# Keys of the first four groups loaded as whole rows, and scores issued one group ahead

## The chip, the cores and the metric

The kernel runs on one core of a Trainium2 chip. The metric is device time in microseconds (us), 1071.01 us before the change: the median of 3 runs.

## The reference, cut to what matters

Chunked attention with 8 memory keys feeds two MLPs, all in float32:

```python
for c in range(24):                                  # chunks of 32 queries, 4 batches, 8 heads
    q_c = q[:, :, 32*c : 32*c + 32]
    k_ctx = k[:, :, max(0, 32*c - 16) : min(768, 32*c + 40)]
    v_ctx = v[:, :, max(0, 32*c - 16) : min(768, 32*c + 40)]
    s = concat([mem_k, k_ctx]) @ q_c / 8             # 8 memory keys, then up to 56 of the context
    a = exp(s - max(s)); a = a / (sum(a) + 1e-9)
    out[:, :, 32*c : 32*c + 32] = a @ concat([mem_v, v_ctx])
x = out as (3072, 512)
h = x @ w_in;   x = (h - tanh(h)) @ w_out            # 512 -> 2048 -> 512
h = x @ w_in2;  g = h if h >= 1, 0 if h <= -1, else (h + 1)**2 / 4;  out = g @ w_out2
```

## The kernel before, in words

**Attention.** The 96 chunks are worked in 24 groups of 4, so a group has 128 queries. For one group, *scores* (`att_scores`, L393) are 64 small matmuls on PE, from queries (128x4x128) and 4 sets of 64 keys. *max* (L411 to L418, DVE) subtracts each row's maximum, *exp* (L428, ACT) follows, *sum* (L445 to L447, DVE) adds up and inverts. *transposes* (L453, PE) and *at* (L458, ACT) turn the probabilities over, *values* (L467, PE) multiplies by V, *norm* (L477, DVE) scales, and *x* (L487, PE) turns the result over into a PSUM tile `start_tx`. From there *xh* (L493, ACT) takes the fp32r high part and *xl* (L498, DVE) the remainder. Scores and values of a group share a PSUM tile `start_a`; transposes and x share `start_tx`.

**Keys.** A chunk's row in DRAM (`qkv_t`) has, for 128 partitions and 4 pairs of heads, 128 keys: 8 memory keys and 120 of the context, of which its own window is the first 64 (8 + 16 + 32 + 8). The rows were laid out with 72 keys to the right, so that a row also holds the windows of the next two chunks, 32 and 64 keys further on. Before, only the first 64 are loaded: one load a chunk, 128 KB, four pieces of 256 bytes a partition (L364).

**The MLPs.** Each matrix product is made of three fp32r products (high times high, high times low, low times high). *hidden* (L563) of one step is 12 matmuls, 4 for each product; *gate* is L576 (ACT) and L577 (DVE); *output* is L601. The weights arrive as float64, a tile of 128x512 pairs of integers (512 KB) in one of four buffers `stage_0` to `stage_3`, and are turned to float32 on the way: *act* (ACT, L138 makes `raw`, L141 shifts the low word), *mag* (DVE, L147 and L148), *sign* (DVE, L156, and the add of POOL, L161), then *whi* (ACT, L173) and *wlo* (DVE, L180). Weight tile 4 goes where tile 0 was, so its load waits for POOL's add of weight 0; tile 5 waits for that of weight 1, and so on.

**The order around the change.** The engines run what they are given in the written order. The *start section* comes first: 11 fills (`warm(WARM, fill)`, L1040: 128x512 bf16 matmuls on zeros into an unused tile), then four groups, one after the other (`for j in range(PER)`, PER = 4), and between their stages the rounding of weights 0 to 3 and more fills (`KEEP`: 6 behind the scores, 2 behind the transposes, 2 behind the values of groups 0 to 2, and the scores of a next group behind its values). In group 3 the first hidden product starts on the 384 columns of groups 0 to 2 (`EARLY_N`), in three parts between the stages of group 3. Behind the start section the main loop takes one hidden step after the other, and group 4 (`att_load`, scores, exp and so on) lies beside its first steps. SP issues all loads in written order: queries and keys of a group, a weight tile, the values, and so on. Each load takes one of 8 semaphores in turn.

## Time and profile before

| what | value |
|---|---|
| runs | 1071.01, 1071.11, 1069.24 us; median 1071.01 |
| span of the profiled execution | 1070.1 us (the page has no time of it beside the span) |
| instructions | 21112 |
| busy | PE 98%, PEld 80%, DVE 80%, ACT 61%, POOL 4% |
| chain that ended last | PE 93%, DMA 2%, SP's queue 2%, ACT 1%, DVE 1% |

The busy share says which engine has no room over the whole span. The chain goes back from the last instruction, at each step to what released it: where it names an engine, that engine's time is in the total; where it names a transfer or a queue, work stood still for it.

### The profile page before, as it was taken

What the parts mean: (1) busy time and instruction counts of PE and PEld (TensorE: products, weight loads), DVE (VectorE), ACT (ScalarE), POOL (GpSimd) and SP (SyncE); (2) the same over time, 40 slices, a digit from 0 to 9 for tenths busy, and PEclk for the clock granted to TensorE, in tenths of its full rate; (3) what the DMA queues carried; (4) which work ended last, traced back from release to release, by engine and by line L of the source; (5) the groups of instructions that cost most, each with busy time, mean ns of one, the idle gap of its engine ahead of it and who ended that gap; (6) DMA issues with size and microseconds to landing.
All of it is one profiled execution on the core that took longest, in us unless ns stands there. A gap on an engine that the chain in (4) does not pass through costs nothing.

```text
span 1070.1 us, 21112 instructions
## 1 busy us (share of the span) xinstructions
PE 1052.4 (98%) x7589; PEld 859.7 (80%) x7589; DVE 855.7 (80%) x1511; ACT 650.0 (61%) x1203; POOL 42.7 (4%) x38
## 2 busy tenths in 40 slices
PE   7799999999999999999999999999999999999998
PEld 3577888888888888888888888888888888888887
DVE  4898987877799999999999778698477787476854
ACT  2687756555455565565566677757477666577553
POOL 0232212000000000000000000000000000000000
PEclk9999999999999999999999999999999999999999
DMA  8999887898889999876487978787766877766774
GB/s 207 245 258 247 260 240 207 258 292 272 266 269 315 325 302 292 292 261 205 154 278 263 313 221 259 210 277 214 232 194 195 261 224 232 214 194 195 203 203 146
DMA packets 212088, 259.37 MB, mean 242 GB/s; under 512 B 65424, under 2 KB 129168, under 8 KB 211984
## 3 DMA queue, kind: packets, MB, share of 16 engines
q1 hardware_dynamic: 211840, 257.88, 80.2%
q8 instruction: 61, 1.00, 0.4%
q14 instruction: 43, 0.35, 0.1%
q10 hardware_dynamic: 144, 0.13, 0.0%
HBM read 199.23 MB, written 58.72 MB: 241 GB/s over the span
## 4 chain that ended last, share of the span: by engine, by line
PE 93%; DMA 2%; SPq 2%; ACT 1%; DVE 1%; issue 0%; ACTq 0%
PE h L563 23%; PE acc L893 21%; PE acc L601 17%; PE qa L805 12%; PE qc L805 6%; PE qb L805 3%; PE acc_-1_1_7132 L893 2%; PE acc_-1_0_7131 L893 2%; DMA stage<-w_in 2%; PE a L467 1%; SPq L364 1%; PE a L393 1%; PE acc_-1_1_7508 L893 1%; PE acc_-1_0_7507 L893 1%; PE b L487 1%; PE b L453 1%
## 5 line engine op out<-in xcount | busy, mean ns | idle before, releaser
L893 PE MATMUL acc<-ghi,inG 128*128 128x512 f32 x672 | 183.0, 389 | 0.0
L576 ACT ACTIVATE g<-h 128x512 f32<-128x512 f32 x96 | 57.7, 601 | 176.7 <-PE h L563 154.9
L893 PEld LDWEIGHTS acc<-ghi,inG 128*128 128x128 f32 x672 | 126.2, 188 | 26.1
L227 DVE TENSOR_TENSOR glo<-g,ghi 128x512 fp32r<-128x512 f32 x174 | 117.8, 688 | 27.4 <-ACT ghi L226 26.3
L805 PE MATMUL qa<-xc,inP 128*128 128x512 f32 x576 | 139.3, 389 | 0.0
L226 ACT ACTIVATE ghi<-g 128x512 fp32r<-128x512 f32 x174 | 107.3, 627 | 43.6 <-DVE glo L227 21.1
L805 PEld LDWEIGHTS qa<-xc,inP 128*128 128x128 f32 x576 | 108.1, 188 | 22.4
L563 PE MATMUL h<-xh,whi 128*128 128x512 f32 (+2 forms) x388 | 105.6, 394 | 3.9 <-DVE g L577 1.9
L893 PE MATMUL acc<-glo,inG 128*128 128x512 f32 x336 | 107.0, 389 | 0.1
L563 PE MATMUL h<-xl,whi 128*128 128x512 f32 (+2 forms) x388 | 104.0, 390 | 0.1
L563 PE MATMUL h<-xh,wlo 128*128 128x512 f32 (+2 forms) x388 | 103.8, 389 | 0.0
L577 DVE TENSOR_TENSOR g<-h,g 128x512 f32<-128x512 f32 x96 | 66.0, 688 | 38.7 <-ACT g L576 38.1
L563 PEld LDWEIGHTS h<-xh,whi 128*128 128x128 f32 x388 | 71.5, 188 | 21.2 <-issue 4.1
L743 ACT ACTIVATE t<-g,half 128x512 f32<-128x512 f32 x72 | 52.2, 725 | 59.1 <-DVE g L739 59.1
L563 PEld LDWEIGHTS h<-xl,whi 128*128 128x128 f32 x388 | 73.0, 189 | 15.2 <-DVE xl L498 0.2
L563 PEld LDWEIGHTS h<-xh,wlo 128*128 128x128 f32 x388 | 72.1, 188 | 14.7
L180 DVE TENSOR_TENSOR wlo<-raw,whi 128x512 fp32r<-128x512 f32 x112 | 80.7, 720 | 0.0
L173 ACT ACTIVATE whi<-raw 128x512 fp32r<-128x512 f32 x112 | 70.5, 630 | 6.5 <-POOL raw L161 6.5
L601 PE MATMUL acc<-ghi,whi 128*128 128x512 f32 x256 | 74.0, 403 | 0.0
L893 PEld LDWEIGHTS acc<-glo,inG 128*128 128x128 f32 x336 | 63.0, 188 | 13.5 <-DVE glo L227 0.5
L805 PE MATMUL qc<-xc,inP 128*128 128x512 f32 x288 | 73.1, 389 | 0.0
L601 PE MATMUL acc<-ghi,wlo 128*128 128x512 f32 x256 | 70.7, 390 | 0.0
(717 smaller groups left out, 1811.3 us busy)
## 6 DMA issues: line engine op xcount, KB each, us to landing
inP<-part SPq DMA_DIRECT2D x168, 256.0 KB, 3.0
inG<-part SPq DMA_DIRECT2D x168, 256.0 KB, 3.0
stage<-w_in SPq DMA_DIRECT2D x32, 512.0 KB, 6.0
stage<-w_out SPq DMA_DIRECT2D x32, 512.0 KB, 5.5
part<-preph SPq DMA_DIRECT2D x64, 256.0 KB, 4.6
whi<-w1o SPq DMA_DIRECT2D x48, 256.0 KB, 4.9
wlo<-w1o SPq DMA_DIRECT2D x48, 256.0 KB, 5.1
part<-prepl SPq DMA_DIRECT2D x48, 256.0 KB, 4.7
```

The costliest lines, as they stand in the source:

```text
L173: nc.scalar.activation(out=hi, in_=r, func=AF.Copy)
L180: nc.vector.tensor_tensor(out=lo, in0=r, in1=hi.bitcast(F32), op=ALU.subtract)
L226: nc.scalar.activation(out=hi, in_=src, func=AF.Copy)
L227: nc.vector.tensor_tensor(out=lo, in0=src, in1=hi.bitcast(F32), op=ALU.subtract)
L364: nc.sync.dma_start(out=k[j // 2][:, j % 2], in_=ks[j, :, :, :WIN])
L563: nc.tensor.matmul(hp, w[:, kc * 128:(kc + 1) * 128], x[:, kc, n0:n1], start=j == 0 and kc == 0, stop=j == 2 and kc == KC - 1,)
L576: nc.scalar.activation(out=g, in_=hp, func=AF.Tanh)
L577: nc.vector.tensor_tensor(out=g, in0=hp, in1=g, op=ALU.subtract)
L601: nc.tensor.matmul(acc_t[dm], w[:, dm * 128:(dm + 1) * 128], g, start=first and j == 0, stop=last and j == 2,)
L743: nc.scalar.activation(out=t, in_=h, func=AF.Relu, scale=0.5, bias=half)
L805: nc.tensor.matmul(o, w[:, k * 128:(k + 1) * 128], z[k], start=i in (1, 2, 5) and j == 0 and k == 0, stop=j == 2 and k == 1, skip_group_ch ...
L893: nc.tensor.matmul(bank[a][c], w[:, c * 128:(c + 1) * 128], g, start=first and j == 0, stop=last and j == 2, skip_group_check=True,)
```

## The change

The loads of keys of groups 0 to 3 are replaced by 6 loads of whole rows (chunks 0, 3, 6, 9, 12 and 15; 256 KB each, 2 KB a partition in one piece). The chunk of a row reads its window in place. For the other ten chunks GpSimd (POOL) copies the 8 memory keys and the 56 context keys out of a row into a set of 64 (`att_windows`, two copies a chunk, 128x4x8 and 128x4x56; sets in `prep0` to `prep4`).

The loop over the four groups is written anew: scores of group j + 1 stand right behind the transposes of group j, its max before the values of j, its exp behind them. There is one tile `start_tx` for all groups instead of one a group, and two `start_a`. Four fills stand behind the values of groups 0 to 2 in the place of ten. Weight 0 is rounded on DVE behind the norm and the xl of group 2, and its whi is made in group 3.

```diff
-KEEP = {"s": 6, "t": 2, "v": 2}
+REACH = (KEYS - WIN) // CHUNK + 1
+KEEP = 4
...
+            att_v(t, (free.pop(0), free.pop(0)))
+            return
+        q = free.pop(0).rearrange("p (j a c) -> p j a c", j=GC, a=NPAIR)
+        nc.sync.dma_start(out=..., in_=qkv[t * GC:(t + 1) * GC, :, :NPAIR * TQ]...)
+        for c in range(t * GC, (t + 1) * GC):
+            if c % REACH == 0:
+                k = free.pop(0)
+                nc.sync.dma_start(out=k, in_=qkv[c, :, NPAIR * TQ:QK])
+                k_rows.append(k.rearrange("p (a c) -> p a c", a=NPAIR))
...
+    def att_windows(t):
+        keys = []
+        for c in range(t * GC, (t + 1) * GC):
+            m, u = divmod(c, REACH)
+            if len(k_win) <= m:
+                k_win.append(slot(f"prep{m}", f"startk{m}").rearrange("p (u a c) -> p u a c", u=2, a=NPAIR))
+            if u:
+                w = k_win[m][:, u - 1]
+                nc.gpsimd.tensor_copy(out=w[:, :, :NMEM], in_=k_rows[m][:, :, :NMEM])
+                nc.gpsimd.tensor_copy(
+                    out=w[:, :, NMEM:], in_=k_rows[m][:, :, NMEM + u * CHUNK:NMEM + u * CHUNK + WIN - NMEM]
+                )
+                keys.append(w)
+            else:
+                keys.append(k_rows[m][:, :, :WIN])
+        st[t]["k"] = keys
...
-    start_scores(0)
+    start_a = [pool.tile([128, 2, 512], F32, tag=tag, name=f"start_a{i}") for i, (pool, tag) in ...]
+    start_tx = ps_acc.tile([128, 2, 512], F32, tag="acc1", name="start_tx")
+    att_windows(0)
+    att_scores(0, start_a[0])
+    att_max(0)
+    att_exp(0)
     for j in range(PER):
         last = j == PER - 1
+        att_transpose(j, start_tx[:, 0, :])
         if not last:
-            warm(KEEP["s"], fill)
-        att_max(j)
-        if j:
-            att_xl(j - 1)
+            att_windows(j + 1)
+            att_scores(j + 1, start_a[(j + 1) % 2])
+        att_at(j)
+        att_sum(j)
         if last:
+            split_weights_hi(0, 0)
+            round_mag(0, 0, 1)
             split_weights_lo(0, 0)
-            hidden(0, 0, EARLY_N, (0,))
-        if 1 < j:
-            round_sign(0, 0, j - 2)
-        att_exp(j)
-        att_sum(j)
-        tx = ps_acc.tile([128, 2, 512], F32, tag="acc1", name=f"start_tx{j}")
-        att_transpose(j, tx[:, 0, :])
-        att_at(j)
-        if j == 2:
-            split_weights_hi(0, 0)
-        if j:
-            round_act(0, 0, j - 1)
-        if last:
-            split_weights_hi(1, 0)
-            hidden(0, 0, EARLY_N, (1,))
+            hidden(0, 0, EARLY_N, (0, 1))
+            round_sign(0, 0, 1)
         else:
-            warm(KEEP["t"], fill)
-        att_values(j, st_pair.pop(j))
+            att_max(j + 1)
+        att_values(j, start_a[j % 2])
         if last:
             hidden(0, 0, EARLY_N, (2,))
         else:
-            warm(KEEP["v"], fill)
-            start_scores(j + 1)
+            att_exp(j + 1)
+            warm(KEEP, fill)
         att_norm(j)
-        if last:
-            split_weights_lo(1, 0)
-        if j:
-            round_mag(0, 0, j - 1)
-        att_x(j, tx[:, 1, :])
+        if j == 2:
+            round_mag(0, 0, 0)
+        att_x(j, start_tx[:, 1, :])
         att_xh(j)
-    att_xl(PER - 1)
-    round_sign(0, 0, 2)
+        if 0 < j:
+            round_act(0, 0, j - 1)
+        att_xl(j)
+        if j == 2:
+            round_sign(0, 0, 0)
+    split_weights_hi(1, 0)
+    split_weights_lo(1, 0)
+    round_rest(0, 0, 2)
     round_act(0, 0, 3)
     round_rest(0, 0, 3)
```

In the rows of order that follow, each instruction stands as line, operation, tile written, tiles read, shape and count; a number in a tile's name is a running number.

SP's queue before, the loads of groups 1 and 2 with their weight tiles (start_151 and start_156 are the queries, the 128x4x64 rows the keys, the 64x2x256 rows the values):

```order
L358 DMA start_151<-qkv_t 128x4x128
L364 DMA start_152<-qkv_t 128x4x64 x2
L364 DMA start_153<-qkv_t 128x4x64 x2
L126 DMA stage_0_180<-w_in 128x1024
L377 DMA start_154<-qkv_t 64x2x256 x2
L377 DMA start_155<-qkv_t 64x2x256 x2
L358 DMA start_156<-qkv_t 128x4x128
L364 DMA start_157<-qkv_t 128x4x64 x2
L364 DMA start_158<-qkv_t 128x4x64 x2
L126 DMA stage_1_191<-w_in 128x1024
L377 DMA start_159<-qkv_t 64x2x256 x2
```
and now (start_152 and start_156 are the rows of keys):

```order
L354 DMA start_151<-qkv_t 128x4x128
L361 DMA start_152<-qkv_t 128x512
L128 DMA stage_0_175<-w_in 128x1024
L407 DMA start_153<-qkv_t 64x2x256 x2
L407 DMA start_154<-qkv_t 64x2x256 x2
L354 DMA start_155<-qkv_t 128x4x128
L361 DMA start_156<-qkv_t 128x512
L128 DMA stage_1_183<-w_in 128x1024
L407 DMA start_157<-qkv_t 64x2x256 x2
L407 DMA start_158<-qkv_t 64x2x256 x2
```
Four loads of keys a group became one (two in groups 0 and 3); everything behind them is nearer to the front by as many places.

DVE before, from xl of group 2 to xl of group 3 (L498; r_587 is the sum, xn_643 the norm of group 3; raw_0 to raw_2 are weights 0 to 2):

```order
L498 TENSOR_TENSOR xl_355<-start_tx_481,xh_354 128x4x128
L180 TENSOR_TENSOR wlo_0_577<-raw_0_381,whi_0_488 128x512
L156 SCALAR_TENSOR_TENSOR raw_1_490<-stage_1_191,raw_1_490 128x512
L445 TENSOR_REDUCE r_587<-e_571 128x8
L446 TENSOR_SCALAR r_587<-r_587 128x8
L447 RECIPROCAL r_587<-r_587 128x8
L477 TENSOR_TENSOR xn_643<-start_a_529,r_587 128x512
L180 TENSOR_TENSOR wlo_1_645<-raw_1_490,whi_1_601 128x512
L147 TENSOR_SCALAR raw_2_598<-raw_2_598 128x512
L148 TENSOR_SCALAR raw_2_598<-raw_2_598 128x512
L498 TENSOR_TENSOR xl_355<-start_tx_591,xh_354 128x4x128
```
DVE now, from xl of group 2 on (r_574 is the sum, xn_631 the norm of group 3; mag of weight 0 stands just ahead of the first row):

```order
L528 TENSOR_TENSOR xl_358<-start_tx,xh_357 128x4x128
L158 SCALAR_TENSOR_TENSOR raw_0_459<-stage_0_175,raw_0_459 128x512
L475 TENSOR_REDUCE r_574<-e_511 128x8
L476 TENSOR_SCALAR r_574<-r_574 128x8
L477 RECIPROCAL r_574<-r_574 128x8
L149 TENSOR_SCALAR raw_1_562<-raw_1_562 128x512
L150 TENSOR_SCALAR raw_1_562<-raw_1_562 128x512
L182 TENSOR_TENSOR wlo_0_582<-raw_0_459,whi_0_578 128x512
L158 SCALAR_TENSOR_TENSOR raw_1_562<-stage_1_183,raw_1_562 128x512
L507 TENSOR_TENSOR xn_631<-start_a_213,r_574 128x512
L528 TENSOR_TENSOR xl_358<-start_tx,xh_357 128x4x128
L182 TENSOR_TENSOR wlo_1_644<-raw_1_562,whi_1_642 128x512
```
Mag and sign of weight 0 moved to either side of xl of group 2; mag of weight 1, wlo of weight 0 and sign of weight 1 stand between the sum and the norm of group 3, and xl of group 3, which stood behind mag of weight 2, now stands right behind the norm, with wlo of weight 1 behind it.

PE before, from x of group 2 (xn_562) to x of group 3 (xn_643); h_579 is the first hidden step, the rows of values are those of 32x64:

```order
L487 MATMUL start_tx_481<-ident,xn_562 128x128 x4
L563 MATMUL h_579<-xh_354,whi_0_488 128x384 x4
L453 MATMUL start_tx_591<-ident,e_571 128x128 x4
L563 MATMUL h_579<-xl_355,whi_0_488 128x384 x4
L467 MATMUL start_a_529<-starty_164,at_596 32x64 x4
...
L467 MATMUL start_a_529<-starty_165,at_596 32x64 x4
L563 MATMUL h_579<-xh_354,wlo_0_577 128x384 x4
L487 MATMUL start_tx_591<-ident,xn_643 128x128 x4
```
and now:

```order
L517 MATMUL start_tx<-ident,xn_553 128x128 x4
L483 MATMUL start_tx<-ident,e_511 128x128 x4
L593 MATMUL h_584<-xh_357,whi_0_578 128x384 x4
L593 MATMUL h_584<-xl_358,whi_0_578 128x384 x4
L497 MATMUL start_a_213<-starty_162,at_572 32x64 x4
...
L497 MATMUL start_a_213<-starty_163,at_572 32x64 x4
L593 MATMUL h_584<-xh_357,wlo_0_582 128x384 x4
L517 MATMUL start_tx<-ident,xn_631 128x128 x4
```
Both parts of the hidden step that read whi_0 (product with xh, product with xl) now stand between the transposes and the values of group 3.

## Rows read from the trace of the kernel before

**Rows 1.** Busy time of each engine by stretch: stretch, its length, then the columns named.
```profile
core 0: us, PE busy (x) PEld busy (x) DVE busy (x) ACT busy (x) POOL busy (x), PEclk, DMA share, GB/s
0.00:49.00 49.00, 37.77 (x697) 23.88 (x697) 29.82 (x57) 19.18 (x33) 7.25 (x11) 0.93 0.89 225
...
60.00:80.00 20.00, 19.98 (x276) 15.96 (x275) 19.16 (x38) 17.84 (x57) 6.60 (x5) 1.00 1.05 264
...
160.00:1000.00 840.00, 839.87 (x5263) 693.84 (x5262) 683.23 (x1203) 517.32 (x911) 6.53 (x5) 1.00 0.80 247
```

**Rows 2.** Chain that ended last, 0 to 55 us: start, length, what.
```profile
39.99 4.93 DMA stage<-w_in
...
44.94 0.69 ACT raw L138
...
53.95 0.86 PE a L467 x53
```

**Rows 3.** Instructions in order of time, DVE, 24 to 46 us: start, length, instruction, [idle before].
```profile
26.70 0.83 DVE L446 TENSOR_SCALAR r<-r 128x8 f32<-128x8 f32 x1
...
30.47 0.69 DVE L411 TENSOR_REDUCE mx<-start_a 128x8 f32<-128x512 f32 x1 [0.82 <-PE start_a L393]
31.20 0.76 DVE L418 TENSOR_TENSOR e<-start_a,mx 128x256 f32<-128x256 f32 x2
...
37.09 0.69 DVE L477 TENSOR_TENSOR xn<-start_a,r 128x512 f32<-128x512 f32 x1 [1.64 <-PE start_a L467]
...
39.16 0.69 DVE L498 TENSOR_TENSOR xl<-start_tx,xh 128x512 fp32r<-128x512 f32 x1
39.77 0.68 DVE L156 SCALAR_TENSOR_TENSOR raw<-stage,raw 128x512 int32<-128x512 int32 x1
...
40.82 1.42 DVE L148 TENSOR_SCALAR raw<-raw 128x512 int32<-128x512 int32 x1
...
43.48 1.47 DVE L180 TENSOR_TENSOR wlo<-raw,whi 128x512 fp32r<-128x512 f32 x1
45.65 0.43 DVE L147 TENSOR_SCALAR raw<-raw 128x512 f32<-128x512 f32 x1 [0.69 <-ACT raw L138]
```

**Rows 4.** Transfers from 2.8 to 6.8 us: packets, MB, share of 16 engines.
```profile
q1 hardware_dynamic: 2613, 0.91, 93.1%
```

**Rows 5.** The same from 640 to 700 us.
```profile
q1 hardware_dynamic: 8632, 14.33, 79.3%
```

**Rows 6.** Instructions in order of time, PE, 15 to 40 us.
```profile
17.39 1.75 PE L1040 MATMUL fill<-zeros 128*128 128x512 bf16 x6 [2.74 <-issue]
...
20.78 1.18 PE L467 MATMUL start_a<-start,at 64*32 64x64 f32 x64
...
29.68 0.76 PE L393 MATMUL start_a<-starty,start 64*32 64x64 f32 x52 [0.43 <-DMA starty<-qkv_t]
...
31.71 1.37 PE L563 MATMUL h<-xh,whi 128*128 128x384 f32 x4 [0.69 <-ACT xh L493]
...
33.58 1.63 PE L563 MATMUL h<-xl,whi 128*128 128x384 f32 x4
...
37.83 0.66 PE L487 MATMUL start_tx<-ident,xn 128*128 128x128 f32 x4
```

**Rows 7.** Busy time by stretch, 19 to 20 and 33 to 34 us (columns as in rows 1).
```profile
19.00:20.00 1.00, 1.00 (x6) 0.88 (x5) 0.00 (x0) 0.00 (x0) 0.00 (x0) 0.50 0.93 160
33.00:34.00 1.00, 1.00 (x6) 1.00 (x5) 1.00 (x3) 0.00 (x0) 0.12 (x1) 0.50 0.94 222
```

**Rows 8.** Instructions in order of time, POOL, 0 to 30 us.
```profile
26.22 1.29 POOL L161 TENSOR_TENSOR raw<-raw,stage 128x512 int32<-128x512 int32 x1 [24.91 <-DMA starty<-qkv_t]
```

**Rows 9.** Groups of instructions of POOL by form: shapes, count, busy us, mean ns, idle.
```profile
masks.py:199 POOL TENSOR_SCALAR_AFFINE_SELECT ident<-ident 128x128 f32<-128x128 f32 x1 | 0.3, 292 | 0.1
```

**Rows 10.** Instructions in order of time, ACT, 36 to 42 us.
```profile
38.53 0.60 ACT L493 ACTIVATE xh<-start_tx 128x512 fp32r<-128x512 f32 x1 [2.28 <-PE start_tx L487]
...
39.58 0.66 ACT L141 ACTIVATE stage<-stage 128x512 int32<-128x512 uint32 x1
```

## The prediction

> **What bounds the kernel now.** I read the busy time by stretch first: from 60 us on PE is busy 19.98 of 20 us, from 160 to 1000 us 839.87 of 840 [rows 1]. Nothing of that work changes, so a gain or loss can only be made before PE is full, and the change lies there: 37.77 of the first 49 us are busy. The chain of waits says from when on nothing is lost: PE's unbroken run in it begins at 53.95, with the values of group 4 [rows 2]. Time won ahead of that point moves the end, time won on anything else does not. The chain names a transfer ahead of it: weight 4 lands at 44.92, ACT makes raw of it at 44.94 [rows 2], DVE its mag at 45.65 [rows 3]. A reader would say that the loads decide and that fewer packets pay in full. The idle time in front of that mag says otherwise: DVE had waited 0.69 us for it [rows 3]. Ahead of it stand DVE's rounding of weights 1 to 3 and group 3, so **faster loads alone give 0.69 us at most; the rest must come from DVE's queue**, which behind this point is the same before and after. So I ask one thing: when does DVE reach the mag of weight 4?

> The queue there has the same instructions on both sides from the norm of group 3 on (wlo 1, mag 2, xl 3, sign 2, mag 3, sign 3, gate, wlo 2), but for one difference: now xl 3 stands ahead of wlo 1 and mag 2. Before, those two filled the time in which x and xh of group 3 ran.

> **Loads of keys.** Removed: 16 loads, 16 x 128 x 4 = 8192 packets of 256 bytes. Where such packets are most of the traffic, 2613 took 0.931 of 16 engines for 4 us [rows 4], 22.8 ns each: 8192 x 22.8 / 16 = 11.7 us of all 16. Added: 6 x 128 = 768 packets of 2 KB. Late in the kernel a packet of 1.66 KB on average took 0.793 x 960 / 8632 = 88 ns [rows 5]; taken as it is or by bytes (109 ns), the rows cost 4.2 to 5.2 us. Saved: 6.5 to 7.5, I take 7.0. By bytes alone it would be (2.10 - 1.57 MB) / 225 GB/s = 2.3 [rows 1], the lower end. The queue was busy 0.89 of the stretch [rows 1] and I let the gaps stand: 7.0 x 0.89 = 6.2 us by the last keys. They reached the scores of group 3 at 29.68, which had waited 0.43 for them [rows 6]; now 23.5, and the row of chunk 12, which has to be copied, one load (0.9) ahead, 22.6.

> **Copies.** 20 on POOL, four a row, 512 elements a partition in all. The trace has none. Nearest below: 128 elements in 292 ns [rows 9], so 1.2 us a row; nearest above: 512 elements with two inputs in 1.29 [rows 8], which gives 1.3 a row by elements and 5.2 if each of the four costs as much. I take 1.2, since the small one is the nearest in kind; bounds 0.3 and 5.2. The first add of POOL, queued behind all 20, comes at about 30 us, when they are long done. Group 3's are not hidden: scores start at 22.6 + 1.2 = 23.8.

> **The chain through group 3.** 52 of 64 matmuls took 0.76 [rows 6], all 0.9: 24.7. From there max and subtraction end 31.20 + 0.76 - 30.44 = 1.5 behind the scores [rows 3, 6]: 26.2. The norm of group 2 is queued behind them, 0.69 [rows 3]: 26.9; x, 0.66 [rows 6]: 27.6; xh, 0.60 [rows 10]: 28.2; xl, 0.69 [rows 3]: 28.9; sign of weight 0, which now stands behind xl, 0.68 [rows 3]: 29.6; POOL's add, 1.29 [rows 8]: 30.9; whi 0, an ACT pass as L141, 0.66 [rows 10]: 31.5. Only now can the hidden parts of 384 columns start; before, they had their whi in time and waited only for xh [rows 6]. They stand ahead of the values of group 3: 1.37 + 1.63 = 3.0 [rows 6], 34.5. Values: 1.18 [rows 6], 35.7; norm 36.4; x 37.1. So xh of group 3 starts at 37.1, not at 38.53 [rows 10]: of 6.2 us, 1.4 are left.

> **Behind it.** ACT takes raw 2 and the shift, which begins 1.05 after xh [rows 10], then whi 1, half a microsecond later and 0.66 long: 39.3. wlo 1 waits for that, and sign 2 is two places on: between norm and xl of group 3 lay norm, wlo 1 and mag 2 in 2.07 us [rows 3], without the norm (0.6 from start to start) 1.5: 40.8, where sign 2 was at 39.77. That is 1.0 later. The waiting for weight 4 goes, 0.69 [rows 3], since its load is no longer late; what is late next is DVE itself. **Sum: +1.0 - 0.69 = +0.3 us.**

> Costed at nothing: PE's idle 2.74 in front of the fill at 17.39 [rows 6], put down to issue, returns in some place; group 2 or 3 waits there for its row anyhow, and if it fell on the chain it would cost up to 2.7. Weight tiles 6 and 7 still wait for POOL's adds of weights 2 and 3, so part of what the queue saves becomes waiting of SP; both stand behind weight 4 in SP's queue and its mag does not need them. Loads of group 4 and the compute of groups 0 to 2 have room. Of the 41 fills 18 go; PE was idle enough that only the clock can notice.

> The sum is made against the profiled span, 1070.1, which lies 0.9 below the median of 1071.01; I put it on the median: 1071.3.

> **Two prices that could be wrong.** [...]

> POOL beside DVE: an addition of 128x8 on DVE took 0.83 us, from 26.70 to 27.53, just past the end of POOL's add from 26.22 on for 1.29 [rows 3, 8]; the mag half at 40.82 took 1.42 and wlo 2 took 1.47, where a mag half takes 0.43 [rows 3]. So one of the two stands still for the other. [...]

> **Rivals.**
> 1. *Faster* (0.30): the saving passes further. For it: the price of 3.0 for the hidden parts and 1.18 for the values is that of the low clock; at the full one they would save 1.9 or so (3.0 and 1.18 halved is the limit, 2.1). The blocks of DVE by POOL (1.42 for 0.43 at 40.82, and 1.47 for some 0.7 at 43.48 [rows 3]) may fall elsewhere: 1.8. The first alone, 1069.4, is still in the forecast's range; both give 1067.6, and 1064.0 comes out if all 7.0 us pass on. Against: whi 0, made so late, stands between the loads and norm 3 in the written order, and DVE's queue decides.
> [...]
> 3. *Slower, by copies* (0.05): each costs 1.3, a row 5.2 instead of 1.2; 4.0 on the chain, 1075.3. It decides from about 3 us a row. Against: the small instruction of POOL [rows 9].
> 4. *The loads don't get faster* (0.05): the row packets cost by bytes only what the small ones did. 2.0 saved instead of 6.2: 1075.5. Against: 22.8 ns for 256 bytes beside 88 for 1.66 KB [rows 4, 5].

> **How the numbers follow.** The forecast has 0.45, with its own range 1069.2 to 1073.4: two terms are each uncertain by about 1 us (the low clock in part, the gaps of the queue), and about 2.1 us, 0.2%, is what a measurement here can tell from none. Faster is rival 1, 0.30; slower rivals 2 to 4, 0.25. For 8 in 10, the lower end takes in two thirds of rival 1 (down to 1066.5, 0.10 left out), the upper end rival 2 with half a microsecond (1074.3, rivals 3 and 4 left out, 0.10).

> **What would show it.** Right: the keys of group 3 in place by 23 to 24.5; whi 0 near 31; hidden parts of 384 columns ahead of the values of group 3; xh of group 3 near 37; no idle time of DVE in front of the mag of weight 4 for the load, that mag within 1 us of 45.65; values of group 4 within 1 us of 53.95, and PE full behind it. [...] If PE's busy stretch began where it did and the time differed by over 2 us, my reading that only the start counts would be wrong.

## The result and the profile after

The changed kernel took 1081.28 us (median of 4 runs, 1078.26 to 1084.10) beside 1070.39 for the kernel before: a ratio of 1.0096, 95% interval 1.0070 to 1.0123. It is slower by some 10 us where the forecast was no difference. The profiled executions, with spans of 1070.1 us for the kernel before and 1082.3 for the changed one, are among the longer of their kernels (18 others of the kernel before had 1066.1 to 1070.6), so the ratios give the size of an effect, and a single profile only its place.

The busy time by stretch, as in [rows 1]:

```profile
0.00:49.00 49.00, 32.00 (x583) 20.07 (x583) 19.34 (x42) 12.23 (x21) 8.20 (x28) 0.69 0.73 189
...
160.00:1000.00 840.00, 839.86 (x5383) 693.81 (x5382) 683.94 (x1206) 515.51 (x910) 9.15 (x7) 1.00 0.80 247
```

From 160 to 1000 us nothing has changed; nearly all of the loss is in the start. In its first 49 us PE is busy 32.00 us where it was 37.77, at a mean clock of 0.69 (0.93 before), and the DMA share fell from 0.89 to 0.73: the queue has less to do, and what was won there is idle.

The loads and copies went nearly as forecast. The last copies of group 3 on POOL (start, length, instruction, idle before):

```profile
23.76 0.21 POOL L375 COPY startk<-start 128x32 f32<-128x32 f32 x1 [4.46 <-DMA start<-qkv_t]
...
24.38 0.37 POOL L376 COPY startk<-start 128x224 f32<-128x224 f32 x1
```

They end at 24.75 (forecast 23.8), and a row's four take 0.99 us (forecast 1.2). The chain that ended last says what came then. Here is its stretch from the values of group 1 to those of group 3 (start, length, what):

```profile
20.11 0.89 PE start_a L497 x57
21.01 0.97 PE fill L1070 x2
21.98 2.20 issue
24.18 1.03 PE fill L1070 x2
25.21 0.87 PE start_tx L517 x4
...
27.48 1.11 PE start_tx L483 x4
28.59 1.12 PE start_a L423 x62
29.71 0.73 PE start_a L497 x48
30.44 3.93 issue
34.37 0.45 PE start_a L497 x11
34.83 1.82 PE fill L1070 x4
36.64 0.87 PE start_tx L517 x4
...
40.91 0.64 ACT whi L175
41.59 2.93 PE h L593 x8
44.52 1.12 PE start_a L497 x61
```

No load stands in it behind 20 us. "Issue" is time in which PE waited for nothing that the profile shows: 2.20 us in the fills ahead of x of group 1, and 3.93 in the middle of the values of group 2. What PE waited for in the first 50 us, by line (us in total, times, longest):

```profile
PE start_tx L483 <- DVE xl L528: 4.2, 3, 1.4
PE start_a L497 <- issue: 3.9, 1, 3.9
...
PE fill L1070 <- issue: 2.2, 1, 2.2
PE h L593 <- ACT whi L175: 1.6, 1, 1.6
```

The transposes of each group wait 1.41 us for xl of the group before, because both use the one tile `start_tx`, and the hidden parts wait 1.57 us for whi of weight 0. And DVE, as in [rows 3], from the norm of group 3 to the mag of weight 4:

```profile
45.67 0.69 DVE L507 TENSOR_TENSOR xn<-start_a,r 128x512 f32<-128x512 f32 x1 [2.58 <-PE start_a L497]
...
51.59 0.69 DVE L158 SCALAR_TENSOR_TENSOR raw<-stage,raw 128x512 int32<-128x512 int32 x1
...
56.70 0.41 DVE L149 TENSOR_SCALAR raw<-raw 128x512 f32<-128x512 f32 x1
```

The mag of weight 4 is at 56.70 where it was at 45.65: 11.05 of the 12.2 us between the two spans are lost by then.

### The profile page after: what moved, and what is told of

Its sections match the earlier page's. It is cut to its first block, busy times and chain, and to the rows that moved or that the text cites. A ratio compares the mean times of both kernels' runs of the same rounds, so it can differ in the third digit from the quotient of the medians.

```text
span 1082.3 us, 21083 instructions
## 1 busy us (share of the span) xinstructions
PE 1055.9 (98%) x7571; PEld 863.4 (80%) x7571; DVE 855.2 (79%) x1511; ACT 649.5 (60%) x1203; POOL 47.5 (4%) x58
## 4 chain that ended last, share of the span: by engine, by line
PE 92%; DVE 3%; ACT 2%; issue 1%; SPq 1%; DMA 1%; POOL 0%; ACTq 0%
PE h L593 22%; PE acc L923 21%; PE acc L631 16%; PE qa L835 12%; PE qc L835 6%; PE qb L835 3%; PE acc_-1_1_7125 L923 2%; PE acc_-1_0_7124 L923 2%; PE a L497 1%; PE a L423 1%; PE acc_-1_1_7501 L923 1%; PE acc_-1_0_7500 L923 1%; ACT e L465 1%; DMA start<-qkv_t 1%; PE b L483 1%
```

## The experiments

Ratios are to the kernel before, run on the same chip, with their 95% intervals.

### The loads alone, the order alone

**e1**: the changed kernel with the loop of the kernel before in the place of the new one.

```diff
-KEEP = 4
+KEEP = {"s": 6, "t": 2, "v": 2}
...
-    att_windows(0)
-    att_scores(0, start_a[0])
...
+    for j in range(PER):
+        att_windows(j)
+    start_scores(0)
...
```

> The new loads and all copies, in the order of the kernel before. Theory A (the new order of the start section costs the 11 us; loads and copies are harmless): 1069.7 to 1071.0 us, PE's unbroken run from 53.3 to 54 us. Theory B (the loads cost it: denser transfers make PE wait for its own code, 2.20 and 3.93 us in the changed kernel, and POOL's copies block DVE): 1074 us or more, with a stall of PE over 2 us behind 20 us.

**e2**: the kernel before with the new loop; its loads of keys stay.

```diff
-    start_scores(0)
...
+    att_scores(0, start_a[0])
+    att_max(0)
+    att_exp(0)
...
```

> The new order with the loads of the kernel before. Theory A: at least as slow as the changed kernel, 1078 to 1088 us, since the keys come later on top of it. Theory B: 1071 to 1074 us.

Measured: e1 1072.17 us, 1.0022 (1.0010 to 1.0033); e2 1081.83 us, 1.0108 (1.0091 to 1.0125). **The order makes the loss**, whichever loads it has: e2 is as theory A gave. e1 lies between the two theories, nearer to A, but with the stall of over 2 us that B named. It gains nothing either, though its keys are there 6 us earlier. PE in e1, the scores of group 3:

```profile
29.96 0.25 PE L423 MATMUL start_a<-start,start 64*32 64x64 f32 x3 [3.09 <-issue]
```

In the kernel before the last of these scores began at 29.68 and had waited for a load [rows 6]; here they begin at 29.96, having waited for nothing shown. DVE's mag of weight 4 comes at 44.94, earlier by 0.71, the 0.69 of the sum, and PE's unbroken run begins at 53.24 instead of 53.95; the time does not show it. In these two profiles the 0.7 us are kept up to the last matmul, which ends 0.8 us earlier, and lost behind it. PE's last matmuls in the kernel before and in e1, whose spans are both 1070.1:

```profile
1066.01 0.39 PE L893 MATMUL acc<-glo,inG 128*128 128x512 f32 x1
```

```profile
1065.20 0.39 PE L923 MATMUL acc<-glo,inG 128*128 128x512 f32 x1
```

From the end of that matmul to the end of the span it is 3.73 us before and 4.49 in e1. In the three kernels with the old loads of keys (before, e2, e15) this end takes 3.72 to 3.73 us, in all fifteen with the new ones 4.19 to 4.54. So the new loads come with 0.5 to 0.8 us more at the end; what makes it longer was not tried. That is less than 0.1%: the rest of what makes e1 0.2% slower is not settled.

### What PE waits for under "issue"

The count of PE's instructions up to the wait tells more than its time. In these rows (columns as in [rows 1]) the two counts in front are the matmuls and the weight loads. The changed kernel, up to the middle of its two waits:

```profile
0.00:22.50 22.50, 16.19 (x349) 8.63 (x349) 8.70 (x21) 5.16 (x8) 4.65 (x22) 0.79 0.93 243
0.00:31.00 31.00, 21.04 (x476) 12.05 (x476) 11.58 (x28) 7.48 (x12) 5.64 (x26) 0.72 0.95 241
```

e1, in its waits of 1.43, 0.98 and 3.09 us:

```profile
0.00:15.00 15.00, 11.57 (x222) 5.46 (x222) 5.31 (x14) 3.40 (x6) 3.69 (x18) 1.00 0.88 238
0.00:20.50 20.50, 15.74 (x348) 7.92 (x349) 8.38 (x20) 5.67 (x9) 4.68 (x22) 1.00 0.94 251
0.00:28.00 28.00, 20.83 (x475) 10.75 (x475) 14.20 (x31) 9.25 (x15) 6.97 (x27) 1.00 0.98 260
```

The kernel before, in its only long one, the 2.74 us ahead of 17.39 [rows 6]:

```profile
0.00:15.00 15.00, 11.12 (x221) 5.54 (x222) 4.51 (x12) 3.03 (x5) 0.70 (x6) 1.00 0.85 205
```

Whatever the order, PE stands still at the same counts. In the changed kernel, e1 and the kernel before they are 443 to 444, 697 to 698 and 950 to 952 matmuls and weight loads. With PE's other recorded instructions counted too, it is 449, 705 and 961, exactly 256 apart, in all of the 18 profiles that wait there (a few less in e9 to e12, which lack some records of matmuls). Ahead of each such wait's end the queue of instructions moves one packet of 0.02 MB, taken here for a block of code. A kernel does not wait at each of these places: the kernel before passed the second at 22.90, 3.9 us behind the start of its block's transfer, and the changed kernel the first at 18.76, 5.6 us behind it, both without a wait. In the changed kernel, transfers from 24.3 to 31.6 us and from 31.6 to 33 us:

```profile
q1 hardware_dynamic: 2835, 1.59, 101.3%
```

```profile
q1 hardware_dynamic: 435, 0.23, 69.4%
q8 instruction: 1, 0.02, 5.3%
```

PE went on at 24.18 behind the first wait, and for 7 us no code came, with the queue of loads full (101.3%); then a block came, and PE went on at 34.37. Two things hold at these three places in all 18 profiles. The block's transfer starts only when PE has passed the place before, 256 instructions back. And PE goes on 2.4 to 2.9 us after the transfer starts (one of 34 waits, the first in e9, had 3.55). So PE stands still where it is through its 256 instructions before the next block is in; from 24.18 to 30.44 it took 6.3 us for them, and the next transfer starts only behind 31.6. The two places cost 2.20 and 3.93 us here. What was left to test is whether a block is late because loads are ahead of it, which is theory Q of the expectations.

**e5**: the changed kernel with the loads of group 4 behind weight tile 4, which waits for POOL's add of weight 0.

```diff
-    att_load(PER)
...
     for j in range(AHEAD):
         load_weights(0, 0, PER + j)
+        if not j:
+            att_load(PER)
```

> The changed kernel, but the loads of group 4 (queries, keys, values) are issued behind weight tile 4, which waits for POOL's add of weight 0, so little is under way from about 27 to 40 us. Theory Q (PE's wait for its code at the 961st instruction, 3.93 us, is the wait of the code's transfer behind the loads): that wait falls below 2 us and the time to 1078 to 1080 us. Theory P (the code comes as late without them): 1081 to 1083 us.

**e9**: the same edit on e1.

> The new loads and copies in the order of the kernel before, and the loads of group 4 issued behind weight tile 4. With the new loads alone the scores of group 3 had waited 3.09 us for their code at the 962nd instruction, so the keys' 6 us were lost there. Theory Q (the code's transfer waits behind the loads): that wait is under 1 us, the mag of weight 4 comes 1.5 to 2.5 us earlier than 44.94, 1066.5 to 1068.5 us, a ratio to before of 0.997 to 0.999. Theory P (the code comes as late without the loads, or DVE is the bound): as with the new loads alone, a ratio of 1.000 to 1.003.

e5: 1078.01 us, 1.0085 (1.0070 to 1.0101), the second wait 1.51 us: both as theory Q gave, though the interval overlaps that of the changed kernel. e9: 1.0013 (1.0003 to 1.0023), the wait 2.27 us, where theory Q asked for less than 1 us and 0.999 at most: missed. The loads of weights 2 and 3 were still under way. So:

**e13** (the changed kernel) and **e14** (e1): weight tiles 2 and 3 and group 4 all behind weight tile 4; **e15**: the same for the kernel before.

```diff
-        if j:
+        if 0 < j < PER - 1:
             load_weights(0, 0, j - 1)
...
-    load_weights(0, 0, PER - 1)
-    att_load(PER)
...
             round_sign(0, 0, 0)
+            load_weights(0, 0, 4, "stage0")
+            load_weights(0, 0, 2, "stage2")
+            load_weights(0, 0, 3, "stage3")
+            att_load(PER)
...
```

> The changed kernel; weight tiles 2 and 3 and the loads of group 4 are issued behind weight tile 4, which waits for POOL's add of weight 0, so next to no loads run from about 25 us to that add. Theory Q (PE's code waits behind the loads): the next block of code starts within 2 us of the wait at the 706th instruction, the wait at the 962nd is under 1 us (3.93 in the changed kernel), and the ratio to before is 1.005 to 1.0075. Theory P: that wait stays 2 to 4 us, ratio 1.008 to 1.011.

> The new loads in the order of the kernel before, with weight tiles 2 and 3 and group 4 behind weight tile 4 (which waits for POOL's add of weight 0 at about 26 us). Theory Q: the wait at the 962nd instruction (3.09 us with the new loads alone, 2.27 with group 4 late) is under 1 us, the mag of weight 4 comes at 41.5 to 43.5 us, ratio 0.996 to 0.999. Theory P: a wait of 2 to 3 us, ratio 1.001 to 1.003.

> The kernel before with that order of its loads alone. Its keys of group 3 are not moved, so by both theories the scores of group 3 start where they did; the values of group 3 no longer wait for their load (0.69 us): ratio 0.9985 to 1.0005. If weight tiles 2 and 3 then come too late for DVE: 1.001 to 1.003.

PE in e13, its two waits for code:

```profile
23.34 0.60 PE L1070 MATMUL fill<-zeros 128*128 128x512 bf16 x2 [2.42 <-issue]
...
29.45 0.45 PE L497 MATMUL start_a<-start,at 64*32 64x64 f32 x11 [0.62 <-issue]
```

Its transfers from 23.4 to 28.2 us:

```profile
q1 hardware_dynamic: 227, 0.20, 15.7%
q8 instruction: 1, 0.02, 1.4%
```

The first wait, with loads around it, stays (2.42, 2.20 before the edit); the second, without, falls from 3.93 to 0.62. In e14 the same place fell from 3.09 to 0.35. So both waits are as short as theory Q asked. **That PE's code waits behind the loads is supported by this, not shown**, for other profiles speak against it. In e4 (below), which has all loads of the changed kernel, the second wait is 1.19 us, and the block came 3.6 us behind the first wait, with the queue full (109.6%). PE's wait, and the transfers from 22.93 to 26.5 us:

```profile
29.06 0.43 PE L497 MATMUL start_a<-start,at 64*32 64x64 f32 x11 [1.19 <-issue]
```

```profile
q1 hardware_dynamic: 576, 0.85, 109.6%
```

In e13 the block came just as late, 3.7 us behind the first wait, not within the 2 us expected, although nothing at all was moved from 25.4 to 27.0 us. And in e16 (below), with the loads of e13, PE waits 1.12 us there, in e12, with group 4 alone late, 0.68. A single profile also says little about a length: up to the first place e1, e9 and e14 run the same, and wait 1.43, 1.68 and 2.60 us. What decides when a block is fetched stays open.

The times: e13 1.0071 (1.0053 to 1.0089), as Q gave, though its interval overlaps that of the changed kernel; e14 0.9999 (0.9988 to 1.0009), not below 0.999, but clear of e1's. Yet PE in e14 is no earlier at the third place:

```profile
16.65 1.25 PE L1070 MATMUL fill<-zeros 128*128 128x512 bf16 x5 [2.60 <-issue]
...
23.68 0.24 PE L423 MATMUL start_a<-startk,start 64*32 64x64 f32 x2 [2.61 <-issue]
...
29.91 0.25 PE L423 MATMUL start_a<-start,start 64*32 64x64 f32 x3 [0.35 <-issue]
```

It goes on at 29.91, e1 at 29.96: the three waits add up to 5.56 and 5.50 us. What differs is the clock behind the third. The stretch from 30 to 37 us in e1, behind a wait of 3.09, and in e14, behind one of 0.35:

```profile
30.00:37.00 7.00, 6.31 (x115) 5.12 (x115) 4.96 (x9) 3.47 (x6) 1.29 (x1) 0.54 0.63 169
```

```profile
30.00:37.00 7.00, 5.78 (x122) 4.15 (x122) 6.76 (x14) 3.85 (x7) 1.30 (x1) 1.00 1.05 319
```

The first hidden part takes 1.65 us in e1 and 0.97 in e14, and the mag of weight 4 comes at 43.37, not 44.94. PE in e14 further on:

```profile
51.81 0.86 PE L497 MATMUL a<-v,at 64*32 64x64 f32 x64 [0.38 <-ACT at L488]
...
65.90 0.31 PE L497 MATMUL a<-v,at 64*32 64x64 f32 x11 [2.39 <-ACT at L488]
```

The 2.1 us won by 51.81 (53.95 before) are lost at 65.90, where at had stood in ACT's queue behind a weight tile that landed late, at 64.13: the loads that were put off are missed there. This execution took 1073.81 us where the median of e14 is 1069.79, so the loss need not be that large in the others. e15 has no key earlier and pays for the delay alone, 1.0018 (1.0008 to 1.0028): its expectation's second case. Beside it e14, with the same delay, is 0.2% faster (the two intervals just touch), which may be what the earlier keys give there.

### The clock and the fills

**e3**: `KEEP = 10`, as many fills in all as before the change. **e7**: `KEEP = 0`.

> The changed kernel with 10 fills a group behind the values in place of 4, as many as before the change (41 in all). If the granted clock is what makes it slow (theory A1): the clock is 1.00 through most of 10 to 48 us, the three hidden parts of 384 columns take about 0.8 each instead of 1.5 to 1.65, some 4 us less, and 6 more fills in front of each x give 1.3 of that back: 1077 to 1079 us. If waits and code stalls are (A2): 1080 to 1084 us, since the fills stand in front of x.

> The changed kernel without the fills behind the values (11 in all, those at the start). Theory A1 (the clock): slower, 1083 us or more, the clock at 0.50 nearly throughout 10 to 48 us. Theory A2 (the fills stand in front of x on PE and cost 1.0 to 1.9 us a group at the low clock): 1077 to 1080 us.

e3: 1084.16 us, 1.0132 (1.0105 to 1.0159). e7: 1078.91 us, 1.0097 (1.0082 to 1.0112), no different from four fills. The stretch from 10 to 48 us in the changed kernel, e3 and e7, one each:

```profile
10.00:48.00 38.00, 25.32 (x504) 17.12 (x504) 16.74 (x35) 9.12 (x16) 5.53 (x14) 0.60 0.75 186
```

```profile
10.00:48.00 38.00, 24.65 (x514) 15.41 (x512) 15.84 (x34) 8.94 (x15) 5.20 (x13) 0.77 0.72 172
```

```profile
10.00:48.00 38.00, 24.69 (x580) 19.07 (x579) 21.36 (x42) 12.92 (x23) 6.90 (x15) 0.61 0.71 185
```

With ten fills a group the clock is 0.77 where it is 0.60 with four, and nothing is gained. The fills stand on PE in front of x, on the chain: ten take 4.38 and 3.78 us there in groups 1 and 2 of e3, four took 2.00 and 1.82. (The intervals of e3 and the changed kernel overlap, so that ten are slower is not shown.) Without any, it is 0.61, the same as with four. With the same four fills, but most of the waiting for xl gone, it is 0.79 (e4, below). In the order of the kernel before, with its 41 fills, it is 0.91 (before and e1) and 0.96 (e14). Of these 38 us PE was busy 24.69 and 25.32 at the clocks of 0.61 and 0.60, 27.34 at 0.79 (e4), and 28.79 to 30.48 at 0.91 to 0.96. So the low clock mostly went with PE's waiting here, though not in e3 (24.65 us busy, 0.77) nor in e13 (28.08, 0.69); what sets it is not shown. Fills between dependent steps did not pay.

### The links of the new order

**e4**: x goes to the tile of its group's scores and values. **e6**: weight 0 rounded behind xl of group 1, its whi behind the exp of group 3. **e8**: both, as below. **e10**: e6 with POOL's copies all queued ahead.

```diff
         if last:
-            split_weights_hi(0, 0)
...
             att_exp(j + 1)
+            if j == 2:
+                split_weights_hi(0, 0)
...
-        if j == 2:
-            round_mag(0, 0, 0)
-        att_x(j, start_tx[:, 1, :])
+        att_x(j, start_a[j % 2][:, 0, :])
...
-        if j == 2:
-            round_sign(0, 0, 0)
+        if j == 1:
+            round_rest(0, 0, 0)
```

> The changed kernel, but x is turned into the tile of its group's scores and values, which is free by then, so the transposes of the next group don't wait for xl. If those three waits (1.41 us of idle PE each) are on the chain, the two of groups 1 and 2 go, 2.8 us: 1078 to 1079 us. If PE's stalls for code or the loads take their place: 1080 to 1082 us.

> The changed kernel, but weight 0 is rounded behind xl of group 1 and its whi made behind exp of group 3, as early as its act allows. If the late whi is on the chain (PE waits 1.57 us for it after the transposes of group 3, and DVE and POOL work on it between xl of group 2 and that point): 2 to 3 us less, 1078.5 to 1079.5 us. If the stalls ahead of it are all: 1081 to 1082 us.

> x in the tile of its group's scores and values, as in the run before with that alone (0.65% slower than the kernel before), and the early rounding of weight 0. If both are links of one chain their gains add: 1073 to 1075 us. If the early rounding gains nothing by itself: 1076 to 1077 us.

> The changed kernel with the early rounding of weight 0 as tried, but POOL's copies of group 3 queued ahead of its add of weight 0, not behind it. If the copies' wait behind that add (1.93 us of idle PE in the scores of group 3) is what limited that run: 2 us less than there, a ratio of 1.005 to 1.006. If PE then waits for its code at that place: a ratio of 1.007 to 1.008.

e4: 1076.49 us, 1.0065 (1.0042 to 1.0089); PE now waits 3.40 us for whi of weight 0, where it waited 1.57. e6: 1076.76 us, 1.0074 (1.0059 to 1.0089). Both are over 1 us below the better of their two cases. e8: 1.0066 (1.0049 to 1.0083), no better than e4. e6 had made a new wait: POOL's add of weight 0 stood ahead of the last four copies. POOL in e6:

```profile
26.97 1.28 POOL L163 TENSOR_TENSOR raw<-raw,stage 128x512 int32<-128x512 int32 x1 [8.22 <-issue]
28.19 0.21 POOL L375 COPY startk<-start 128x32 f32<-128x32 f32 x1
```

and PE in e6, the scores of group 3:

```profile
28.77 0.78 PE L423 MATMUL start_a<-startk,start 64*32 64x64 f32 x6 [1.93 <-POOL startk L376]
```

With the copies ahead, e10 is at 1.0060 (1.0047 to 1.0073), though PE then waits 2.82 us for code in the values of group 2. So the shared tile and the late weight 0 are each worth some 0.3%, but neither is shown by itself: the intervals of e4 and e10 still overlap that of the changed kernel.

**e11**: e4 and e10 with group 4 late as in e5. **e12**: e11 and the order of the kernel before behind the values of group 3. **e16**: e12 with the loads of e13.

```diff
             round_sign(0, 0, 1)
+            round_act(0, 0, 2)
+            split_weights_hi(1, 0)
...
         att_norm(j)
+        if last:
+            split_weights_lo(1, 0)
+            round_mag(0, 0, 2)
```

> The changed kernel with x in its own tile, the early rounding of weight 0, all copies at the front of POOL's queue, and the loads of group 4 late. If each removes a link of the chain: 1.001 to 1.003. If only one of them can count (something else ends at the same place): 1.005 to 1.007.

> The run before, and behind the values of group 3 the order of the kernel before: raw 2 and whi 1 ahead of xh of group 3 on ACT, wlo 1 and mag 2 ahead of xl of group 3 on DVE. If that order costs the 2.5 to 3.2 us between the norm of group 3 and the mag of weight 4 that the changed kernel loses there: 0.0023 to 0.003 less in the ratio than the run before, so 0.998 to 1.001. If DVE's work behind it is the bound: the same as the run before.

> The changed order with all repairs tried (x in its own tile, early rounding of weight 0, copies in front, the order behind group 3 of the kernel before), and the loads of weight tiles 2 and 3 and of group 4 behind weight tile 4. Theory Q: better than the same repairs with group 4 alone late (1.0032): 0.999 to 1.002. Theory P, or a bound behind group 3 (loads of group 5): 1.002 to 1.004.

In the changed kernel these steps (act and mag of weight 2, whi and wlo of weight 1) stand behind xh of group 3 or behind the loop. e11: 1.0037 (1.0024 to 1.0050), between its two cases and clear of the changed kernel: the repairs add up, to less than their sum. e12: 1.0032 (1.0019 to 1.0044); the order behind group 3 showed no gain that can be told from none. e16: 1.0030 (1.0021 to 1.0040), the same, and more than the 1.002 that theory Q allowed. So some two thirds of the loss are taken back, and what is left is near that of e1. No version beats the kernel before; e14 equals it.

## Why the prediction was wrong

| step | forecast, us | measured, us |
|---|---|---|
| copies of group 3 done | 23.8 | 24.75 |
| scores of group 3 done | 24.7 | 29.7 |
| norm of group 2 begins | 26.2 | 34.90 |
| xh of group 2 begins | 27.6 | 37.53 |
| whi 0 begins | 30.9 | 40.91 |
| values of group 3 begin | 34.5 | 44.45 |
| xh of group 3 begins | 37.1 | 47.81 |
| sign 2 begins | 40.8 | 51.59 |

**Right**: the loads and copies (the row of chunk 12 there at 23.76 for 22.6, the copies done 1.0 us late), the copies' price, the reading that the start decides (0.8 us more stand behind the last matmul, as in e1), and the way behind group 3: from xh to sign 2 forecast 3.7 us, measured 3.78; from sign 2 to the mag of weight 4, 5.11 where it had been 5.88, 0.77 less, the slack of 0.69. That faster loads alone give 0.69 at most fits e1: 0.71 at the mag in its profile, and nothing in its time.

**Wrong**, as the table shows, between the keys and the norm of group 2, by 8.7 us less the 1.0 of the keys; behind it the lateness stays, at 9.9 to 10.8. The scores of group 3 ended 4.95 us behind the copies, not 0.9, because the fills and x of group 1 and the transposes stand ahead of them on PE and were late; the norm of group 2 began 5.2 us behind those scores, not 1.5, and 3.93 of it is one wait. The step that failed is the one "costed at nothing": that the compute of groups 0 to 2 has room, and that PE's idle 2.74 us would fall where "group 2 or 3 waits there for its row anyhow". It took the loads for the bound of that stretch because the kernel before waits for keys there. With the keys early, the next bound was PE's own path: waits for xl (1.41 a group, by e4 worth some 0.3%), and its code, 2.20 and 3.93 on the chain. I had read the 2.74 as a sum that occurs once; it was one of a series at fixed places in the program, 256 instructions apart. e11, which goes at the shared tile, the late whi and the loads of group 4 together, takes back 0.6 of the 1.0%. How much of the loss the waits for code make is not shown (e11's profile still has 3.75 and 1.47 us of them), and a third of it is left unexplained.

**The late whi 0** was counted in the chain, with its price: right in kind, and early rounding gave some 0.3% back (e10). I did not set against it what an earlier one would give.

**The low clock.** The upper end of the range holds 2.5 us for PE at a low clock through group 3 (rival 2: 1073.8 instead of 1071.3), and the forecast's own range counts it in part; no run shows that price, and that fewer fills bring the clock down was the author's estimate. The side of rival 2 came, and from x of group 2 to x of group 3 the clock is 0.50:

```profile
36.44:47.01 10.57, 7.59 (x86) 6.08 (x84) 5.52 (x10) 2.94 (x5) 2.57 (x2) 0.50 0.30 84
```

But fewer fills are not what made the time longer: with none the time is the same, and with ten it is no better (1078.91 us in e7 and 1084.16 in e3, 1081.28 with four). What the low clock costs by itself no run isolates. Rivals 3 and 4 are out by the copies' 0.99 us and the keys' landing. Rival 1 needed the saving to pass on; the profiles of e9 and e14 show a part that does, 1.7 and 2.1 us by the start of PE's run, and their times (1.0013, 0.9999) show no gain.

The range ended at 1074.3 because its upper end held, beside the price of the low clock, only known waits at known prices. A stall put down to "issue", unexplained, in the rows that the sum is made from, is a price to be bounded from above, as often as its place can recur. One reading was loose without effect: the sum sets the profiled span of 1070.1 beside times, but a time is some 1.8 us longer than its span (1084.10 and 1082.3 for the changed kernel).

## What to carry to other kernels

Before earlier loads are counted as won time, follow what the waiting engine would do next with nothing to wait for: its program order, the tiles it shares, and its own code. Count the instructions up to each unexplained wait: here such waits lay at the same counts in every version (443 to 444, 697 to 698 and 950 to 952 matmuls and weight loads), nearly all with a packet of the instruction queue 2.4 to 2.9 us ahead of their end, and so they were read as waits for code. To learn what makes one of them long, take more than one profile of a version, since the length at one place differed by over 1 us between kernels that are the same up to there. Moving a step ahead in one queue (weight 0's add on POOL, for which PE waited 1.93 us in e6) is only safe after a look at what stands behind it there.
